# Decay steps pass one wait more in each mixing step, and half of the early head transfers are issued by GpSimd

## The chip, the cores and the metric

The kernel runs on one core of a Trainium2 chip. The metric is the device time of one execution in microseconds (us), and less is better. Three executions before the change took 908.11, 912.96 and 916.42 us; their median is 912.96 us.

## The reference

For 4 batches, 8 heads, 768 positions and a head size of 48, the reference runs a gated linear recurrence and then two token-and-channel mixers.

```python
mag = sqrt(a_re**2 + a_im**2)
scale = minimum(mag, 0.999) / (mag + 1e-6)            # a = a_re + i*a_im, times scale
for t in range(768):                                  # for each batch and head
    S_re, S_im = (Re(a_t * S) + outer(k_t, v_t), Im(a_t * S))
    y[t] = q_t @ S_re
x = y as [batch, 768, 384]
h = relu(x^T @ w_tok1) @ w_tok2;  u = x + h^T          # token mixing
u = u + relu(u @ w_ch1) @ w_ch2                        # channel mixing, first set
xn = (u - mean) / sqrt(var + 1e-6) * g
out = u + relu(xn @ w_ch1') @ w_ch2'                   # channel mixing, second set
```

## The kernel before

The recurrence is not run position by position. The running product of the decays is formed as a magnitude and an angle, and q and k are multiplied with it, so that each head becomes a few matmuls over chunks of 128 positions.

**Decay work** (`Piece`, driven by `gen_E`). The 384 rows (8 heads times 48) of a batch are three row tiles of 128 rows, and a piece is one row tile over one half of the positions. A piece goes through F (the magnitude; its first instruction is the Square of L228), G and H (running product, q and k scaled), T1 and T2 (running angle, sine and cosine) and T3. Nearly all of it is 384 columns wide: VectorE (DVE) through the recorder of L172, ScalarE (ACT) through `act` of L198, and three-element copies on GpSimd (POOL), L274 and L320 to L325. T3 ends with the transfers to the heads: rows of the piece are copied by DMA into the head tiles `stk`, one transfer from `R` (L338; named t, u or w in the trace) and one from `qkt` (L339; named qk or u). A row tile overlaps three or four heads, so a piece issues three or four pairs. All of them stand in the queue of SyncE (SP).

**Heads** (`gen_P`). A head comes in three parts: transposes of k (L507) and the first half of the scores (L520); the second half and the sums for the state (L547, scanned at L548); the output (L567 to L579). The results are split into two half-precision numbers (`xh`, `xl`, L475 and L476).

**Mixing** (`gen_M`). For each batch: `tok1` (with two `relu_split`, L670 on ACT and L672 on DVE), `tok2` (six chunks, each with an ACT and a DVE eviction, L721 and L722, and a Square, L725), then two rounds of `mlp(wm1)` and two of `mlp(wm2)`, 12 steps each. A step is 18 matmuls of 384 columns (`mm3`, L662 to L664) and one `relu_split`, so there are 198 of the L670 activations: 48 steps in each batch and two for each of three `tok1`.

**What sets the order.** The main loop takes one mixing step, then lets the decay work of the next batch run (`run_E`), and then up to two head parts (`run_P`). `run_E` has a budget, and it also stops at every "wait" that the decay generator yields; a piece yields seven of them. At the end of a batch all head parts of the next batch are forced out ahead of its `tok1`, with whatever decay work they need. The tile framework then arranges the emitted instructions on each engine by a timeline of its own, and each engine executes in that order. `tc.issue_after` adds an edge to that arrangement. The same framework gives DMAs their semaphores. `tokw` (L679) fetches the token weights of the next batch from POOL's queue as soon as the buffers are free.

Of the kernel before, what the change touches and what calls it, by code (L numbers as in the profile page):

```python
# [21 lines left out]
P = 128  # L22
# [16 lines left out]
def tile_kernel(ctx: ExitStack, tc: tile.TileContext, a_in, qk_in, v_in, aq2_in, v2_in, wt_in, wm1_in, wm2_in, w64_in, g_in, c_in, out):  # L39
# [150 lines left out]
    def act(**k):  # L190
        s = "trig" if k["func"] in (AF.Sin, AF.Arctan) else "logs"
        if tab["set"] != s:
            with ExitStack() as gates:
                for x in tab["ops"]:
                    gates.enter_context(tc.issue_after(x))
                tab.update(set=s, load=A.preload_act_table_set(sets[s]).ins, ops=[])
        with tc.issue_after(tab["load"]):
            tab["ops"].append(A.activation(**k).ins)  # L198

    class Piece:  # L200
# [21 lines left out]
        def F(self):  # L222
# [5 lines left out]
            A.activation(out=self.sq.rearrange("p (x s) -> p x s", x=2), in_=self.both, func=AF.Square)  # L228
# [84 lines left out]
        def T3(self, qkt):  # L313
# [12 lines left out]
            for k in range(self.n):  # L326
# [6 lines left out]
                while r < P:  # L333
# [5 lines left out]
                    nc.sync.dma_start(out=stk[b, h][D + d0:D + d0 + m, hf], in_=qkt[r:r + m, k])  # L339
# [5 lines left out]
    def gen_E():  # L345
        qks = [load_qk(0, j // 2, j % 2) for j in range(6)]
        load_w(1)
        ps = [[Piece(0, i, hf) for hf in range(2)] for i in range(3)]

# [98 lines left out]
    def gen_P(alt):  # L448
# [30 lines left out]
        for n, (b, h) in enumerate(heads):  # L479
# [20 lines left out]
            A.activation(out=dr.rearrange("p e (y c) -> p e y c", y=2), in_=kq[:, :, 2 * HB:].unsqueeze(1).to_broadcast([2 * D, D, 2, 3]), func=AF.Copy)  # L500
# [3 lines left out]
            for half in range(2):  # L504
                if half == 0:
                    for c in range(5):
                        T.transpose(tr[:, c * 96:(c + 1) * 96], qc(c, 1), eye[0:96, 0:96])  # L507
                    kTc = A.activation(out=kT, in_=tr[:, 0:480].rearrange("p (c d) -> p c d", c=5), func=AF.Copy, scale=(VS * SS if n in YS else 1.0) / (QS if n in QZ else 1.0))
# [16 lines left out]
                ev = V.tensor_tensor(out=sT[half], in0=sc[:, 0:3 * P].rearrange("p (c t) -> p c t", c=3), in1=pair(mask, 3), op=ALU.mult)  # L525
# [169 lines left out]
    def tok1_half(g, r1):  # L695
# [3 lines left out]
        for j in range(2):  # L699
# [4 lines left out]
            A.activation(out=r1[j][:, 0, cs], in_=p[:, j], func=AF.Relu, accum_out=hstat[:, n_h[0]:n_h[0] + 1])  # L704
# [320 lines left out]
    st = {"phase": "", "alt": True, "e": 0, "p": 0, "pp": 0, "w": 0, "need": 0, "c": 0, "mk": 0}  # L1025
# [24 lines left out]
    def run_E(budget, until=None):  # L1050

        if until is None and budget < 0:
            return
        while st["e"] < 3 * B and (until is None or st["e"] < until):
# [63 lines left out]
    for b in range(B):  # L1118
        k = 0
        while True:  # L1120
# [20 lines left out]
            run_E(EB if b else EB0 if k <= KE else EB1)  # L1141
# [38 lines left out]
PADB = 0  # L1180
PIPE = 0
# [38 lines left out]
EB = 2200  # L1220
# [5 lines left out]
NSTK = 5  # L1226
YS = [n for n in range(32) if n >= YH or n in YX]
# [51 lines left out]
```

## Time and profile before

| | |
|---|---|
| runs | 908.11, 912.96, 916.42 us |
| profiled execution | 912.68 us, its span 910.9 us |
| mean granted TensorE clock | 0.96 of full speed |
| PE busy | 816.8 us (90% of the span) |
| DVE busy | 631.2 us (69%) |
| ACT busy | 606.2 us (67%) |
| POOL busy | 97.8 us (11%) |

The profiled execution is one of its own, 0.28 us under the median of the runs. PE is TensorE's matmul side; its busy time counts a matmul as long at half clock as it lasts there, so that a busy PE at a granted clock of 0.50 does half of the work. The clock has two levels, 1.2 and 2.4 GHz, shown as 0.50 and 1.00 of full speed. ACT and DVE instructions overlap at their edges, so the distance between two starts on a full engine is a little under the duration of one.

### The profile page before, as it was taken

Reading aid. Unit: us, or ns where it says so; the run is one execution under the profiler, and the core shown is the slowest. Engines: PE = TensorE matmul, PEld = TensorE weight load, DVE = VectorE, ACT = ScalarE, POOL = GpSimd, SP = SyncE. Lnnn points to the kernel's source line nnn. Section 1 sums busy time; section 2 is a strip of 40 time slices with the busy share of each in tenths; the row PEclk is TensorE's granted clock in tenths of the full one; section 3 lists DMA queues with packets and bytes.
Section 4 is the critical chain, followed back from the end, with each engine's and each line's share of the span. In section 5 each row is a group of like instructions: output and inputs, shape, how many; then the busy total and the mean of one; then the engine's idle time right before and its main releaser. Section 6 shows DMA issues by size and latency. Waiting matters only on the chain.

```text
span 910.9 us, 15777 instructions
## 1 busy us (share of the span) xinstructions
PE 816.8 (90%) x5802; PEld 551.3 (61%) x5802; DVE 631.2 (69%) x1094; ACT 606.2 (67%) x1631; POOL 97.8 (11%) x171
## 2 busy tenths in 40 slices
PE   0079898999989999999999988999999999999996
PEld 0068775555757676666567755666567766655563
DVE  6786479998888988426789987336889642364533
ACT  8787147785578996627879996627779934464642
POOL 0421020311011001000020103000020000011110
PEclk9977799999999899999999986999999999999999
DMA  8634684155742642101524141100403011465662
GB/s 302 190 105 125 169 296 140 53 157 153 218 155 68 196 139 82 48 2 45 147 60 145 41 129 47 53 14 14 131 27 117 27 37 60 143 203 196 201 223 97
DMA packets 41606, 108.28 MB, mean 119 GB/s; under 512 B 5904, under 2 KB 23824, under 8 KB 41520
## 3 DMA queue, kind: packets, MB, share of 16 engines
q1 hardware_dynamic: 31936, 56.72, 20.9%
q0 software_dynamic: 9584, 50.47, 17.3%
q8 instruction: 47, 0.77, 0.4%
q14 instruction: 39, 0.32, 0.1%
HBM read 77.20 MB, written 11.01 MB: 97 GB/s over the span
## 4 chain that ended last, share of the span: by engine, by line
PE 34%; ACT 6%; DVE 6%; SPq 2%; issue 1%; DMA 1%; DVEq 0%; ACTq 0%
PE m L663 10%; PE m L664 10%; PE m L662 10%; ACT t L198 1%; PE sc L520 1%; DVE t L172 1%; DVE qk L172 1%; ACT hid L670 1%; SPq L338 1%; SPq L339 1%; PE tr L547 1%; DVE aj L172 1%; DVE xc L780 1%; DMA stk<-t 1%; PE m L719 0%
## 5 line engine op out<-in xcount | busy, mean ns | idle before, releaser
L672 DVE SCALAR_TENSOR_TENSOR hid<-m,hid 128x384 f16<-128x384 f32 x198 | 109.4, 554 | 149.2 <-ACT hid L670 148.6
L662 PE MATMUL m<-u,w 128*128 128x384 f16 x576 | 188.1, 327 | 1.4 <-DVE u L722 0.8
L663 PE MATMUL m<-u,w 128*128 128x384 f16 x576 | 188.0, 326 | 0.0
L664 PE MATMUL m<-u,w 128*128 128x384 f16 x576 | 188.0, 326 | 0.0
L670 ACT ACTIVATE hid<-m 128x384 f16<-128x384 f32 x198 | 95.5, 483 | 138.5 <-PE m L664 137.8
L663 PE MATMUL m<-hid,w 128*128 128x384 f16 x540 | 177.6, 329 | 3.0 <-DVE hid L672 2.7
L664 PE MATMUL m<-hid,w 128*128 128x384 f16 x540 | 177.6, 329 | 0.0
L662 PEld LDWEIGHTS <-w 128*128 128x128 f16 x1176 | 116.1, 99 | 84.6 <-issue 15.2
L664 PEld LDWEIGHTS <-w 128*128 128x128 f16 x1176 | 116.6, 99 | 80.2 <-issue 10.6
L663 PEld LDWEIGHTS <-w 128*128 128x128 f16 x1176 | 116.3, 99 | 76.3 <-issue 4.9
L662 PE MATMUL m<-hid,w 128*128 128x384 f16 x540 | 131.6, 328 | 9.1 <-ACT hid L670 8.3
L172 DVE SCALAR_TENSOR_TENSOR t<-t 128x384 f32<-128x384 f32 x80 | 44.1, 555 | 16.7 <-ACT t L228 12.0
L520 PE MATMUL sc<-stk 96*128 96x128 f32 x300 | 46.1, 288 | 1.6 <-DVE r L525 1.6
L595 POOL DMA_DIRECT2D raw<-in_wm x48 | 25.6, 534 | 174.9 <-DVE sq L640 83.2
L520 PEld LDWEIGHTS sc<-stk 96*128 96x128 f32 x300 | 41.5, 200 | 3.7 <-DVE r L525 1.8
L641 ACT ACTIVATE sq<-sq 128x768 f16<-128x768 uint8 x28 | 23.6, 843 | 28.4 <-DVE sq L640 28.4
L507 PE MATMUL m<-cst,stk 96*128 96x96 f32 x10 | 2.1, 348 | 45.0 <-DMA stk<-qk 45.0
L198 ACT ACTIVATE t<-t 128x384 f32<-128x384 f32 x80 | 40.6, 514 | 0.3
L615 ACT ACTIVATE w<-raw 128x768 f16<-128x768 f32 x28 | 25.3, 904 | 22.2 <-DVE raw L613 22.2
L670 ACT ACTIVATION_READ_ACCUMULATOR hid<-m 128x1 f32 x198 | 38.5, 195 | 0.0
L172 DVE TENSOR_TENSOR qk<-qk,t 128x768 f32<-128x768 f32 x40 | 38.1, 955 | 0.5
L612 DVE SCALAR_TENSOR_TENSOR pad<-raw 128x768 uint8<-128x768 uint8 x28 | 29.0, 1034 | 11.6 <-DMA raw<-in_wm 9.3
(281 smaller groups left out, 1713.7 us busy)
## 6 DMA issues: line engine op xcount, KB each, us to landing
raw<-in_wm POOLq DMA_DIRECT2D x48, 768.0 KB, 4.8
qk<-in_qk SPq DMA_DIRECT2D x23, 384.0 KB, 4.0
aj<-in_a SPq DMA_DIRECT2D x9, 768.0 KB, 5.0
stk<-t SPq DMA_DIRECT2D x40, 144.6 KB, 3.2
stk<-qk SPq DMA_DIRECT2D x40, 144.6 KB, 3.0
raw<-in_wt SPq DMA_DIRECT2D x6, 768.0 KB, 4.5
v<-in_v SPq DMA_DIRECT2D x32, 144.0 KB, 2.4
x_d<-xc SPq DMA_DIRECT2D x24, 192.0 KB, 3.5
```

Source lines behind the costliest of these rows:

```text
L172: r = getattr(nc.vector, n)(*a, **k)
L198: tab["ops"].append(A.activation(**k).ins)
L520: last = T.matmul(sc[:, (c % 3) * P:(c % 3 + 1) * P], qc(c, 1), qc(c, 0), start=True, stop=True)
L595: (nc.sync if n < NSY else nc.gpsimd).dma_start(out=raw.bitcast(U8), in_=w_src[n].bitcast(U8)[:, 3:3 + 8 * S])
L612: V.scalar_tensor_tensor(out=pad[0].bitcast(U8).rearrange("p (a b) -> p a b", b=4)[:, :, 3], in0=byte, scalar=3, in1=byte, op0=ALU.logical ...
L615: wact[n] = A.activation(out=dst[:, :, 0], in_=w, func=AF.Copy, scale=WS).ins
L641: A.activation(out=t[:, HB:2 * HB].bitcast(F16), in_=bad_, func=AF.Copy, accum_out=wstat[:, n:n + 1])
L662: T.matmul(out_, wh, xh_, start=first, stop=False)
L663: T.matmul(out_, wh, xl_, start=False, stop=False)
L664: T.matmul(out_, wl, xh_, start=False, stop=last)
L670: A.activation(out=hl[:, 0], in_=p, func=AF.Relu, accum_out=hstat[:, n_h[0]:n_h[0] + 1])
L672: last[:] = [V.scalar_tensor_tensor(out=hl[:, 1], in0=p, scalar=0.0, in1=hl[:, 0], op0=ALU.max, op1=ALU.subtract).ins]
```

## The change

Three settings differ; the other new names (`HOLD`, `AHOLD`, `FE`, `EBA`, `AHEAD`, `RW2`) have values under which the code does what it did.

- `EW = 2`: in the mixing of batches 1 and later, `run_E` stops at the second "wait" of a step, not at the first. The budget (2200) is as before. During the mixing of batch 0 it stops at the first.
- `DQ = ((0,0),(0,1))`: for row tiles 0 and 1 of batch 0 the transfers from `qkt` are issued by POOL. These are 6 and 8 transfers. Those from `R` stay on SP.
- `GSQ = 1`: in pieces of batches 1 to 3 the first Square of F is arranged behind the last activation that went through `act`.

```diff
@@ def F(self): @@
-            A.activation(out=self.sq.rearrange("p (x s) -> p x s", x=2), in_=self.both, func=AF.Square)
+            with tc.issue_after(tab["ops"][-1]) if b and GSQ else ExitStack():
+                A.activation(out=self.sq.rearrange("p (x s) -> p x s", x=2), in_=self.both, func=AF.Square)
@@ def T3(self, qkt): @@
-                    nc.sync.dma_start(out=stk[b, h][D + d0:D + d0 + m, hf], in_=qkt[r:r + m, k])
+                    (nc.gpsimd if (b, i) in DQ else nc.sync).dma_start(out=stk[b, h][D + d0:D + d0 + m, hf], in_=qkt[r:r + m, k])
@@ def run_E(budget, until=None): @@
+        waits = EW if st["bb"] else 1
...
             elif x == "wait":
-                if until is None:
+                waits -= 1
+                if until is None and waits <= 0:
                     return
@@ main loop @@
     for b in range(B):
         k = 0
+        st["bb"] = b
@@ settings @@
+GSQ = 1
...
+EW = 2
+DQ = ((0,0),(0,1))
```

The number of instructions of each kind on each engine is the same, 14 DMAs of SP being POOL's; what changes is their order. Three places show it. Lines of the changed kernel are some 3 to 15 higher than those of the kernel before (L670 is L685, L198 is L199, L339 is L342).

**ACT at the end of batch 1's mixing**, the rows up to the two `relu_split` of batch 2's `tok1` (`hid`). Before, its last twelve rows:

```order
L528 ACTIVATE hl<-r 128x384
L540 ACTIVATE junk,qstat<-qh 96x384
L528 ACTIVATE hl<-r 128x384
L475 ACTIVATE xh<-y 128x6x48
L540 ACTIVATE junk,qstat<-qh 96x384
L553 ACTIVATE junk,qstat<-vh 96x288
L515 ACTIVATE vh<-v 128x288
L551 ACTIVATE vh<-U 96x288
L477 ACTIVATE junk,ustat<-y 128x288
L537 ACTIVATE qh<-stk 96x768
L670 ACTIVATE hid,hstat<-m_6759 128x384
L670 ACTIVATE hid,hstat<-m_6760 128x384
```

and now, from the `relu_split` of the last mixing step on:

```order
L685 ACTIVATE hid,hstat<-m_6978 128x384
L522 ACTIVATE kT<-tr 128x480
L543 ACTIVATE hl<-r 128x384
L685 ACTIVATE hid,hstat<-m_7013 128x384
L685 ACTIVATE hid,hstat<-m_7014 128x384
```

Before, 43 activations (12 of decay, 31 of heads) stand between the last mixing step's `hid` and the first one of `tok1`; now two do.

**ACT and POOL at `tok2` of the next batch**, ACT from the second `hid` of batch 2's `tok1` on (`u` are the six evictions of `tok2`, `junk,ustat<-u` their Squares). Before:

```order
L670 ACTIVATE hid,hstat<-m_6760 128x384
L721 ACTIVATE u<-m_6819 128x384
L725 ACTIVATE junk,ustat<-u 128x384
L721 ACTIVATE u<-m_6837 128x384
L725 ACTIVATE junk,ustat<-u 128x384
L721 ACTIVATE u<-m_6855 128x384
```

and now:

```order
L736 ACTIVATE u<-m_7073 128x384
L740 ACTIVATE junk,ustat<-u 128x384
L231 ACTIVATE t<-aj 128x768
L199 ACTIVATE t<-aj 128x384 x2
L736 ACTIVATE u<-m_7091 128x384
L199 ACTIVATE t,rstat<-t 128x384
L199 ACTIVATE t<-t 128x384
L199 ACTIVATE t,rstat<-t 128x384
L740 ACTIVATE junk,ustat<-u 128x384
L736 ACTIVATE u<-m_7109 128x384
```

Up to the second mixing step's `hid`, 20 decay activations and three more of heads stand there beside the 18 of before. It is the same at `tok2` of batch 1: 19 decay activations, none before. On POOL the fetches of token weights stood next to each other; around batch 1's `tok2` there is now decay work between and behind them:

```order
L694 DMA tokw<-tokw_d 128x3072
L277 TENSOR_TENSOR pstat<-aj,t 128x3
L323 COPY t<-pstat 128x3
L323 COPY qk<-pstat 128x3
L277 TENSOR_TENSOR pstat<-aj,t 128x3
L327 COPY t<-pstat 128x2
L327 COPY qk<-pstat 128x2
L694 DMA tokw<-tokw_d 128x3072
L328 MEMSET t 128x1
L328 MEMSET qk 128x1
```

**SP and POOL at the start**, the transfers of row tile 0 (two halves) to heads 0 to 2 (`stk` twice, then `w`). SP before:

```order
L338 DMA stk<-t 48x771 x2
L338 DMA w_333<-t 32x771
L339 DMA stk<-qk 48x771 x2
L339 DMA w_333<-qk 32x771
L338 DMA stk<-t 48x771
L339 DMA stk<-qk 48x771
L338 DMA stk<-t 48x771
L339 DMA stk<-qk 48x771
L338 DMA w_333<-t 32x771
L339 DMA w_333<-qk 32x771
```

Now SP has the six of `t` alone, and POOL has, behind the three-element copies of that tile:

```order
L327 COPY qk<-pstat 128x2
L342 DMA stk<-qk 48x771 x2
L342 DMA w_333<-qk 32x771
L342 DMA stk<-qk 48x771 x2
L342 DMA w_333<-qk 32x771
```

## Rows read from the trace of the kernel before

**Rows 1.** The page, busy time by engine: us, share of the span, instructions

```profile
PE 816.8 (90%) x5802; PEld 551.3 (61%) x5802; DVE 631.2 (69%) x1094; ACT 606.2 (67%) x1631; POOL 97.8 (11%) x171
```

**Rows 2.** Stretches: length; PE, PEld, DVE, ACT, POOL busy; clock; DMA share; GB/s

```profile
45.00:156.10 111.10, 96.01 (x656) 80.74 (x657) 80.23 (x127) 63.47 (x154) 17.78 (x29) 0.83 0.56 172
239.50:348.70 109.20, 104.00 (x779) 76.60 (x779) 93.84 (x160) 91.05 (x242) 9.90 (x24) 0.95 0.49 143
357.70:373.60 15.90, 15.01 (x154) 11.08 (x153) 10.43 (x20) 11.69 (x36) 0.54 (x1) 1.00 0.38 117
373.60:478.30 104.70, 102.76 (x662) 62.97 (x661) 64.41 (x114) 63.46 (x180) 5.83 (x9) 1.00 0.20 60
478.30:539.50 61.20, 58.93 (x527) 42.45 (x525) 55.85 (x99) 60.96 (x174) 3.73 (x11) 1.00 0.38 108
539.50:565.50 26.00, 20.92 (x156) 14.91 (x156) 21.28 (x39) 20.64 (x65) 8.23 (x6) 0.61 0.11 35
565.50:577.80 12.30, 12.21 (x125) 8.32 (x121) 5.33 (x10) 9.47 (x31) 1.12 (x2) 1.00 0.35 112
577.80:740.60 162.80, 160.81 (x1236) 105.33 (x1234) 104.28 (x184) 113.41 (x336) 6.60 (x10) 1.00 0.17 49
740.60:749.40 8.80, 8.72 (x54) 5.04 (x52) 3.44 (x7) 1.03 (x4) 0.00 (x0) 1.00 0.15 58
```

**Rows 3.** Single stretches, columns as above

```profile
41.00:45.00 4.00, 0.02 (x1) 0.05 (x1) 0.51 (x1) 3.14 (x7) 0.00 (x0) 1.00 1.02 193
...
60.00:80.00 20.00, 19.15 (x101) 16.86 (x101) 14.84 (x24) 13.86 (x30) 3.81 (x8) 0.57 0.52 134
...
536.00:540.00 4.00, 2.19 (x15) 1.29 (x14) 2.79 (x6) 4.00 (x14) 0.00 (x0) 1.00 0.64 199
...
588.00:611.40 23.40, 23.40 (x146) 14.09 (x144) 4.49 (x9) 4.65 (x16) 0.00 (x0) 1.00 0.00 1
```

**Rows 4.** ACT in order of time, full: start, duration, line, operation

```profile
545.26 0.52 ACT L540 ACTIVATE junk<-qh 96x384 bf16<-96x384 f16 x1
...
545.78 0.51 ACT L528 ACTIVATE hl<-r 128x384 f16<-128x384 f32 x1
546.19 0.51 ACT L198 ACTIVATE t<-aj 128x384 f32<-128x384 f32 x1
```

**Rows 5.** Start of the program in order of time; brackets: idle before, releaser

```profile
40.56 0.96 DVE L172 TENSOR_TENSOR qk<-qk,t 128x768 f32<-128x768 f32 x1
...
41.54 0.53 SPq L338 DMA_DIRECT2D stk<-t  x1
...
42.98 0.50 SPq L339 DMA_DIRECT2D stk<-qk  x1
...
44.98 0.71 PE L507 MATMUL m<-cst,stk 96*128 96x96 f32 x3 [44.98 <-DMA stk<-qk]
```

**Rows 6.** Groups by line: busy, mean ns, idle before and releasers

```profile
L228 ACT ACTIVATE t<-aj 128x768 f32<-128x768 f32 x20 | 16.8, 840 | 11.7 <-DMA stk<-t 9.4 <-issue 1.0 <-DMA w<-t 0.9
```

**Rows 7.** SP in order of time, row tile 1's first and last of 16 transfers

```profile
65.66 1.78 SPq L338 DMA_DIRECT2D w<-u  x3
...
75.12 0.59 SPq L339 DMA_DIRECT2D w<-qk  x1
```

**Rows 8.** DMA issues: KB each, median us to landing

```profile
stk<-qk SPq DMA_DIRECT2D x40, 144.6 KB, 3.0
tokw_d<-w POOLq DMA_DIRECT2D x4, 384.0 KB, 2.7
```

**Rows 9.** Line 595: durations in ns, min/median/max, first and last start

```profile
L595 POOL DMA_DIRECT2D raw<-in_wm x48: 528/531/557, 26.5 to 889.7; - x48
```

**Rows 10.** POOL in order of time

```profile
56.70 2.95 POOL L320 COPY qk<-pstat 128x3 f32<-128x3 f32 x1
...
59.86 0.19 POOL L324 COPY w<-pstat 128x2 f32<-128x2 f32 x1
...
370.26 0.54 POOL L679 DMA_DIRECT2D tokw<-tokw_d  x1 [12.80 <-PE m L664]
```

More of the change, by code (lines that the diff above doesn't have):

```diff
@@ L359, in gen_E @@
             qk = qks[2 * i:2 * i + 2]
+            if i == 1 and FE & 1:
+                for x in each(p.F() for p in ps[2]):
+                    yield x
+            if i == 2 and FE & 2:
+                early.extend(Piece(1, 0, hf) for hf in range(2))
+                for x in each(p.F() for p in early):
+                    yield x
             for x in each(p.G() for p in ps[i]):
@@ L422, in gen_E @@
             for i in range(3):
-                ps = [Piece(b, i)] if WIDE else [Piece(b, i, hf) for hf in range(2)]
-                for x in run(p.F() for p in ps):
-                    yield x
+                ps = early if early and (b, i) == (1, 0) else [Piece(b, i)] if WIDE else [Piece(b, i, hf) for hf in range(2)]
+                if ps is not early:
+                    for x in run(p.F() for p in ps):
+                        yield x
                 qk = load_qk(b, i)
@@ L499, in gen_P @@
                 dr = ap.tile([2 * D, D, NCH], F32, tag="dr", name="dr", bufs=1)
-            A.activation(out=dr.rearrange("p e (y c) -> p e y c", y=2), in_=kq[:, :, 2 * HB:].unsqueeze(1).to_broadcast([2 * D, D, 2, 3]), func=AF.Copy)
+            with after(AHOLD.get(n)):
+                A.activation(out=dr.rearrange("p e (y c) -> p e y c", y=2), in_=kq[:, :, 2 * HB:].unsqueeze(1).to_broadcast([2 * D, D, 2, 3]), func=AF.Copy)
             tr = ps_(2)
@@ L507, in gen_P @@
                         T.transpose(tr[:, c * 96:(c + 1) * 96], qc(c, 1), eye[0:96, 0:96])
[L508 removed]
+                    with after(AHOLD.get(n)):
+                      kTc = A.activation(out=kT, in_=tr[:, 0:480].rearrange("p (c d) -> p c d", c=5), func=AF.Copy, scale=(VS * SS if n in YS else 1.0) / (QS if n in QZ else 1.0))
                     if n in YS:
@@ L524, in gen_P @@
                     sT.append(ap.tile([P, 3, P], F32, tag="sT", name="sT", bufs=NST))
-                ev = V.tensor_tensor(out=sT[half], in0=sc[:, 0:3 * P].rearrange("p (c t) -> p c t", c=3), in1=pair(mask, 3), op=ALU.mult)
+                with after(HOLD.get((n, half))):
+                  ev = V.tensor_tensor(out=sT[half], in0=sc[:, 0:3 * P].rearrange("p (c t) -> p c t", c=3), in1=pair(mask, 3), op=ALU.mult)
                 if n in YS:
@@ L1082, in run_P @@
             run_E(0, until=tiles_for(st["p"]))
+            for key in (HOLD.get((st["p"], 0)), HOLD.get((st["p"], 1)), AHOLD.get(st["p"])):
+                while key and key not in fin:
+                    x = nxt(E, "E")
+                    if isinstance(x, tuple) and x[0] == "done":
+                        st["e"] = x[1] * 3 + x[2] + 1
             st["pp"] += 1
@@ L1180 @@
 PADB = 0
+HOLD = {}
+AHOLD = {}
+RW2 = (2, 3) + tuple(range(8, 16))
+AHEAD = lambda n: min(15, n + 4) if 7 <= n < 12 else 3 if n < 2 else n + 1
+DQ = ()
+EW = 1
+EBA = 2200
+KA = 0
+FE = 0
+GSQ = 1
 PIPE = 0
```

15 lines of the change are left out of this document (9 added, 6 removed).

## The prediction

> **What bounds the kernel now.** The busy table on the page comes first [rows 1]: TensorE's matmul side (PE) is busy for 816.8 us of 910.9, the next engine, DVE, for 631.2. The change neither adds nor removes an instruction, so PE's work stays; only time in which PE is idle or at half clock can be won. The windows by stage show where that lies [rows 2]. Most of it is at the start (45 us without a matmul, then 15 us idle in 45 to 156), which decay work must feed, and in one place late: 539.5 to 565.5, the first `relu_split` pair of batch 2's token mixing (`tok1`). There PE is busy 20.92 of 26.0 us at a mean clock of 0.61, which is 20.92 x 0.61 = 12.8 us of full-speed work. The same step of batch 3 lasts 8.80 us with 8.72 busy. The mixing around it (577.8 to 740.6) loses 2 us in 163.
>
> Why there: from 478.3 to 539.5 ACT is busy 60.96 of 61.2 us [rows 2], and the ACT rows follow each other every 0.41 to 0.52 us, decay (L198) and heads (L528, L540) in turn [rows 4]. The decay of batch 2 is behind at the end of batch 1's mixing, and all of the rest, with the head parts that hang on it, is pressed ahead of `tok1`. From 536 to 540 PE is busy 2.19 of 4 us while ACT is busy 4.00 [rows 3], still at clock 1.00; a mean of 0.61 over the 26 us that follow means about 20 us at the lower level, 1.2 GHz. Earlier in a batch's mixing there is room: a stretch without head parts, 588 to 611.4, has ACT busy for 4.65 of 23.4 us [rows 3]. With a second wait in each step decay moves ahead into such steps.
>
> **The change part by part.** The sum goes against the profiled execution, 912.68 us, 0.28 below the median of the three runs.
>
> EW = 2, the pressed place. By the order, 43 ACT instructions stood between the last mixing step and `tok1` of batch 2; two do now. If the 26.0 us shrink to their full-speed work, the gain is 26.0 - 12.8 = 13.2. If only the idle 5.1 goes and the low clock stays, it is 5.1. The head matmuls that leave this place run elsewhere at full clock, so I don't take the 8.8 us of the twin as the goal. I take **-13** (bounds -13.2 and -5.1), since every stretch with PE at 98% or more in [rows 2] stands at clock 1.00. The stretch ahead, 478.3 to 539.5, has 2.3 us idle with ACT full; it has 34 decay and head activations fewer (decay 54 to 43, heads 57 to 34): **-1** (0 to -2.3). From 577.8 to 740.6 2.0 idle: **-1** (0 to -2).
>
> EW = 2 in batch 1's decay, 239.5 to 348.7. ACT is busy 91.05 and DVE 93.84 of 109.2; PE's 104.0 at clock 0.95 is 98.8 of work, 10.4 lost. By the order, 15 decay instructions of ACT and 10 of DVE fewer stand ahead of batch 1's `tok1`. At the spacing of 0.5 us of [rows 4] that is 7.5 us of ACT. **-4**, half, as neither engine is full (0 to -7.5).
>
> What receives the work. At `tok2` of batch 2 ACT has 41 instructions where it had 18. Its stretch, 565.5 to 577.8, has ACT at 9.47 of 12.3 us; 23 more at 0.46 are 10.6, so 20.1 of ACT beside PE's 12.21. If no matmul of heads moves in, that is 7.9 more; if enough do, nothing is lost. At `tok2` of batch 1 (357.7 to 373.6: ACT 11.69, PE 15.01) 19 decay activations come in, 8.7 at 0.46, so 20.4 against 15.9: 4.5. Bounds 0 and +12.4 for both. I take **+4**, nearer to none: the mixing of [rows 2] from 577.8 on carries ACT at 113.4 of 162.8 at a loss of 1%. The evictions L721 stand behind decay there, and PE waits for their PSUM buffers. On POOL the decay's `pstat` and its copies now stand behind the `tokw` fetches, of which one waited 12.80 us for PE [rows 10]; the decay instructions that need them are late by up to that, which costs only where heads wait. [...]
>
> The steps behind it, 373.6 to 478.3: ACT has 25 decay and 53 head instructions more, 78 x 0.51 = 39.8 on 63.46: 103.3 of 104.7. The head matmuls that come with them lengthen the stretch and shorten a later one. PE may wait at some steps: **+2** (0 to +5; the upper end is the idle time of PE, 5.2 of 109.2, where ACT and DVE are both loaded, 239.5 to 348.7).
>
> DQ, the start. Row tile 0's second half is ready when DVE's `qk` ends at 41.52; SP issues its first `qk` transfer at 42.98, behind others, and the first matmul starts on its landing, 44.98 [rows 5]. POOL's DMA instructions take 528 to 557 ns, 48 of them [rows 9], so POOL could issue it at 41.6, 1.4 us sooner. But from 41 to 45 the DMA engines are full, share 1.02 [rows 3]: there the queue that issues is not all of the limit. Landings from both queues are alike, 2.7 us for 384 KB from POOL and 3.0 for 144.6 KB from SP [rows 8]. Row tile 1's 16 transfers hold SP from 65.66 to 75.71 [rows 7]; with eight gone SP ends about 5 us sooner. In 60 to 80 PE is busy 19.15 of 20, at clock 0.57 [rows 3], so it waits for little. On the other side, POOL's transfers stand behind its own three-element copies, of which one took 2.95 us where others take 0.19 [rows 10]. Bounds -6.4 (1.4 + 5) and +6 (two such copies). **-2**.
>
> Added edge (GSQ). The 20 Squares of L228 waited 11.7 us in all, 9.4 of it for transfers (`stk<-t`) [rows 6], with ACT's queue held behind them. Behind the last activation they no longer go ahead of work that is ready; at most 9.4 comes free, and ACT is the limit only in the places counted above. A Square that is late delays its own piece; the next wait is then DVE's for it. **0**, its bounds within those of the terms above.
>
> Sum: -13 - 1 - 1 - 4 - 2 + 4 + 2 = **-15**, so 912.7 - 15 = **898 us**.
>
> **The rivals.**
>
> *The pressure only moves (no net change).* What is won at `tok1` of batch 2 is given back at `tok2` of both batches and in the steps behind: +12.4 and +5 in place of +4 and +2: 912.7 - 13 - 8 + 17.4 = **909**, up to 917 if the first term is only -5. For it: PE is at 98% in 373.6 to 478.3 and at 99% in 565.5 to 577.8, so decay put there has only little slack. Against it: PE has 13 us to recover at one place, and ACT room of 41 us in the stretch that receives most.
>
> [...]
>
> *GpSimd's issues are starved.* The copy of 2.95 us ran beside busy DVE. If each moved transfer took as long to issue, row tile 0's first head would start at 39.6 + 4 x 2.95 + 2 = 53.4 in place of 45, and row tile 1's last issue would end at 67.5 + 8 x 2.95 = 91 in place of 75.7. The first is lost whole, +8; of the second's +15 half, as PE has 19.15 of 20 us of work there: 898 + 2 + 15.5 = **916**. Against: none of the 48 POOL DMA instructions took over 557 ns [rows 9]. The Trainium skill, "SBUF — State Buffer", in its box on the "DVE blocks DMA" trap, states a rule against this edit: a DMA issued from GpSimd has its descriptors written by that engine's cores, and these are locked out while DVE runs an operation in a 2-port performance mode, which float32 tensor copies in SBUF trigger; the page advises the SP or ACT queue. By that rule the time would be near this rival's; the rows on POOL's own DMAs don't show it, though DVE is busy 69% of the span.
>
> *The change hardly does what it says.* EW counts waits, and the budget of 2200 may end a step first; the pressed place stays at 540. The order speaks against it (43 to 2). With the start's -2 alone, 911.
>
> **How the numbers follow.** Two runs of this kernel differ by up to 0.9%, so 1% (9.1 us, 903.8 to 922.1) is what can be told from no change. The forecast's case has 0.63. Its terms' distances to their ends, taken as independent, add (root of the sum of squares) to 7 us below 898 and 15 above; what lies beyond 908 is left to the rivals, so it is 891 to 908, 0.51 of it below 903.8 and 0.12 above. No net change 0.15; starved issues 0.05; `tok2` pressed once 0.05 and at both 0.10; no effect 0.02. Faster by over 1%: **0.51**. Within: 0.12 + 0.15 + 0.05 + 0.05 + 0.02 = **0.39**. Slower: **0.10**. Range **887 to 918**: the forecast's case with 4 us more at its low end, and all cases but the slower one, which leaves out that 0.10 and the edges.
>
> **What would show it.** Right: the clock stays at 1.00 from batch 1's last step through batch 2's `tok2`, and the `tok1` stretch lasts 9 to 15 us with no decay rows of ACT in it; both `tok2` stretches stay under 20 us; the first matmul starts at 43 to 46; POOL's DMA instructions on L342 last about 0.53 us. Wrong: a mean clock under 0.9 in either `tok2`; L736 waited for behind L199; POOL's DMA instructions at 2 us or more; a 26 us stretch with clock 0.6 elsewhere. Most of all, if head parts now run short of PE work earlier in batch 1 and the clock falls there, the 13 us are not won but moved.

## The result and the profile after

The changed kernel takes 898.12 us, the median of 20 runs (891.73 to 909.39); the kernel before takes 910.78 over 20 runs of its own (903.80 to 916.42). The ratio is 0.9861, with a 95% interval of 0.9841 to 0.9881. One of the changed kernel's runs, the 909.39, counts as slow and is left out of the ratio. The gain is 12.7 us, and the forecast of 898 us held.

The profiled execution of the changed kernel is its fastest, 891.73 us with a span of 889.9, while that of before is 1.9 us above its median. Of the 21 us between the two traces some 8 are therefore not the change's. A second trace of each kernel (e7 and e8 below: 899.02 and 913.35 us) shows in which stretches executions of one program differ.

The page of the changed kernel, busy time by engine, answers to [rows 1]:

```profile
PE 799.5 (90%) x5802; PEld 539.2 (61%) x5802; DVE 629.7 (71%) x1094; ACT 603.8 (68%) x1631; POOL 102.2 (11%) x185
```

PE's busy time is 17.3 us lower at the same number of matmuls: fewer of them ran at half clock.

The stages are cut below at the `relu_split` activations on ACT (`hid`), which are the same 198 in every kernel. They are numbered from 0: batch 0's mixing steps are 0 to 47, `tok1` of batch 1 is 48 and 49, batch 1's steps are 50 to 97, `tok1` of batch 2 is 98 and 99, batch 2's steps begin at 100. So the pressed place of the prediction ends at hid 98, and the two `tok2` lie between hids 48 and 50 and between 98 and 100. Windows of the changed kernel between hids 0, 16, 46, 48, 50, 70, 96, 98, 100 and 146, each with its length, busy time of PE, PEld, DVE, ACT and POOL (instructions), mean granted clock, DMA share and GB/s; the first row runs from 45 us to hid 0, and steps 0 to 16 are left out:

```profile
45.00:137.50 92.50, 81.73 (x611) 70.45 (x612) 71.50 (x112) 54.09 (x129) 17.20 (x36) 0.87 0.60 192
190.50:328.70 138.20, 133.73 (x959) 94.21 (x958) 121.08 (x202) 107.26 (x275) 18.61 (x34) 0.98 0.46 140
328.70:344.20 15.50, 13.97 (x108) 9.55 (x107) 13.55 (x26) 13.11 (x34) 0.38 (x3) 1.00 0.70 210
344.20:363.90 19.70, 15.00 (x157) 11.35 (x156) 19.40 (x35) 19.02 (x52) 6.02 (x8) 1.00 0.19 64
363.90:430.60 66.70, 65.61 (x446) 41.32 (x445) 47.68 (x84) 49.38 (x144) 2.94 (x8) 1.00 0.27 82
430.60:533.10 102.50, 98.63 (x825) 67.10 (x824) 88.64 (x157) 95.25 (x273) 12.56 (x18) 1.00 0.31 88
533.10:543.00 9.90, 9.90 (x64) 6.08 (x62) 4.93 (x10) 2.15 (x8) 0.00 (x0) 1.00 0.17 47
543.00:562.10 19.10, 16.51 (x163) 12.47 (x161) 14.36 (x29) 16.24 (x48) 1.31 (x4) 1.00 0.40 122
562.10:716.60 154.50, 154.42 (x1190) 100.71 (x1189) 91.23 (x161) 98.37 (x302) 4.27 (x8) 1.00 0.13 39
```

The same windows of the kernel before, cut at the same hids:

```profile
45.00:147.70 102.70, 88.56 (x611) 76.37 (x612) 71.83 (x115) 56.41 (x135) 17.25 (x28) 0.82 0.56 172
198.50:344.10 145.60, 138.25 (x979) 97.07 (x978) 128.67 (x213) 114.18 (x290) 15.67 (x36) 0.96 0.50 149
344.10:356.10 12.00, 11.47 (x86) 7.53 (x85) 11.04 (x20) 7.89 (x24) 3.12 (x6) 1.00 0.00 1
356.10:371.90 15.80, 14.91 (x156) 11.51 (x155) 11.47 (x23) 11.04 (x31) 1.12 (x2) 1.00 0.31 92
371.90:433.10 61.20, 61.20 (x404) 37.33 (x402) 26.82 (x47) 30.07 (x95) 0.00 (x0) 1.00 0.11 37
433.10:534.70 101.60, 98.70 (x775) 67.04 (x774) 90.62 (x160) 91.22 (x251) 9.36 (x18) 1.00 0.36 102
534.70:565.00 30.30, 23.90 (x170) 16.61 (x169) 24.66 (x45) 24.95 (x76) 8.43 (x8) 0.66 0.18 56
565.00:576.20 11.20, 11.11 (x120) 7.72 (x119) 4.77 (x9) 8.40 (x25) 1.12 (x2) 1.00 0.28 79
576.20:737.70 161.50, 159.51 (x1227) 104.56 (x1226) 104.28 (x184) 114.42 (x340) 6.60 (x10) 1.00 0.18 53
```

Lengths alone mislead, since head matmuls moved from one stretch to another. What can be compared is the time lost to PE: length less busy time times clock. It is an estimate, since the clock is the mean of the whole stretch, to two decimals. In the pressed place before (seventh row) it is 30.3 - 23.9 x 0.66 = 14.5 us; now 9.9 - 9.9 = 0. The place with a clock of 0.66 is gone, and from hid 46 to 146 no stretch is under 1.00.

Two windows of the changed kernel's second trace (e7), from 45 us to hid 0 and from hid 16 to 46:

```profile
45.00:142.60 97.60, 85.41 (x611) 72.74 (x612) 71.67 (x112) 54.41 (x129) 17.24 (x36) 0.84 0.58 183
195.80:335.50 139.70, 134.99 (x959) 95.27 (x958) 121.15 (x202) 107.18 (x275) 18.66 (x34) 0.96 0.45 139
```

and of the second trace of before (e8):

```profile
45.00:144.50 99.50, 85.20 (x611) 74.02 (x612) 71.49 (x114) 56.97 (x134) 17.28 (x28) 0.85 0.59 180
195.30:344.20 148.90, 140.25 (x981) 98.27 (x978) 128.89 (x213) 114.67 (x291) 15.70 (x36) 0.95 0.48 145
```

By the same working the first stretch loses 21.4 and 25.9 us in the two traces of the changed kernel and 30.1 and 27.1 in those of before: executions of one program differ there by 3 to 4.5 us. Between hids 16 and 46 they differ by 2.4 us (7.8 and 10.2) and 3.3 us (12.4 and 15.7). These four, and the column 16-46 further down, are sums over hids 16 to 32 and 32 to 46; the single rows above give 7.1, 10.1, 12.9 and 15.7, so up to 0.7 us of them is rounding. Behind hid 50 the two traces of each program agree in lost time to 0.2 us in every stretch. A difference of single traces counts as shown below only behind hid 46, or where it is well over 4 us.

At the start, the first matmul and the second half's transfers on POOL ahead of it (start, duration, engine, line; in brackets the idle time before and what ended it):

```profile
41.82 1.00 POOL L342 DMA_DIRECT2D stk<-qk  x2 [1.31 <-issue]
...
45.62 0.71 PE L520 MATMUL m<-cst,stk 96*128 96x96 f32 x3 [45.62 <-DMA stk<-qk]
```

The second half's transfer was issued 1.16 us sooner than in [rows 5], at 41.82, and the first matmul that waits for it came 0.64 us later, at 45.62: the earlier issue bought no earlier landing. The traces of the other runs agree. In the seven traces that have row tile 0's transfers on POOL the first matmul starts 2.9 to 3.9 us after that issue, at 45.5 to 46.4; in the seven that have them on SP 2.0 to 2.6 us after it, at 45.0 to 47.7. All 14 transfers of row tiles 0 and 1 on POOL, grouped by line (durations in ns, least, median, most):

```profile
L342 POOL DMA_DIRECT2D w<-qk x10: 488/504/524, 40.0 to 70.1; - x10
L342 POOL DMA_DIRECT2D stk<-qk x4: 502/513/550, 39.0 to 42.3; - x4
```

They take what [rows 9] gave, so none of the 14 issues was lengthened. The Trainium skill, "SBUF — State Buffer", in its box on the "DVE blocks DMA" trap, would have their descriptors held up while DVE runs in a 2-port mode, which a float32 copy in SBUF triggers. This trace hardly tests that rule: DVE ran beside 2.7 of the 7.2 us that the 14 issues took, and what it ran there were TENSOR_TENSOR instructions of two inputs, no copy. What did change is the time from issue to landing. Row tile 1's eight transfers from `qkt` have a median of 4.6 us here, and of 3.6 to 4.6 in all seven traces that have them on POOL; in the seven that have them on SP it is 2.6 to 2.7. SP's own eight beside them rise as well, from 2.7 in before to 3.4 here. Whether POOL's queue is slower or only more is under way at once stays open.

ACT at `tok2` of batch 2 in the changed kernel, in order of time, behind the first eviction (546.57) and its Square:

```profile
548.98 0.84 ACT L231 ACTIVATE t<-aj 128x768 f32<-128x768 f32 x1 [1.28 <-DMA stk<-t]
549.73 0.92 ACT L199 ACTIVATE t<-aj 128x384 f32<-128x384 f32 x2
550.56 0.47 ACT L736 ACTIVATE u<-m 128x384 f16<-128x384 f32 x1
```

The second eviction (L736) stands behind a Square that waits 1.28 us for a transfer, and behind the decay activations after it. PE's waits in this stretch and in that of batch 1 (344.2 to 363.9) by what ended them (us in all, times, longest) are

```profile
PE m L677 <- DVE u L737: 1.4, 2, 0.7
PE sc L534 <- DVE r L540: 1.2, 1, 1.2
```

and

```profile
PE m L677 <- DVE u L737: 3.6, 3, 1.7
PE m L677 <- DVE hid L687: 1.1, 1, 1.1
```

L737 is the DVE half of the same eviction, which follows ACT's. The two stretches lose 4.7 us at batch 1 and 2.6 at batch 2, and of that the evictions are 3.6 and 1.4. At batch 2 DVE's half waits for ACT's, 0.64 us at the second eviction. At batch 1 no such wait shows: the first three DVE halves start 0.7 to 1.9 us after ACT's half has ended, behind decay and head work on DVE itself. So there the evictions stand behind decay on both engines.

### The profile page after: what moved, and what is told of

It reads as the page before. It is cut to its first block, busy times and chain, and to the rows that moved or that the text cites. A ratio compares the mean times of both kernels' runs of the same rounds, so it can differ in the third digit from the quotient of the medians.

```text
span 889.9 us, 15744 instructions
## 1 busy us (share of the span) xinstructions
PE 799.5 (90%) x5802; PEld 539.2 (61%) x5802; DVE 629.7 (71%) x1094; ACT 603.8 (68%) x1631; POOL 102.2 (11%) x185
## 4 chain that ended last, share of the span: by engine, by line
PE 41%; ACT 10%; DVE 5%; DMA 2%; issue 1%; SPq 1%; DVEq 0%; ACTq 0%
PE m L678 12%; PE m L677 12%; PE m L679 12%; ACT t L199 2%; DMA stk<-t 1%; ACT hid L685 1%; PE sc L534 1%; PE tr L562 1%; DVE xc L795 1%; DMA v<-in_v 1%; DVE t L172 1%; DVE hid L687 1%; ACT junk L740 1%; DVE qk L172 1%; ACT t L300 0%
## 5 line engine op out<-in xcount | busy, mean ns | idle before, releaser
L685 ACT ACTIVATE hid<-m 128x384 f16<-128x384 f32 x198 | 95.5, 483 | 122.7 <-PE m L679 121.9
L534 PE MATMUL sc<-stk 96*128 96x128 f32 x300 | 44.3, 282 | 1.2 <-DVE r L540 1.2
L610 POOL DMA_DIRECT2D raw<-in_wm x48 | 25.6, 533 | 166.2 <-DVE sq L655 86.6
L520 PE MATMUL m<-cst,stk 96*128 96x96 f32 x10 | 2.1, 348 | 45.6 <-DMA stk<-qk 45.6
L199 ACT ACTIVATE t<-t 128x384 f32<-128x384 f32 x80 | 40.8, 515 | 1.2 <-DVE t L172 0.9
L277 POOL TENSOR_TENSOR pstat<-aj,t 128x3 f32<-128x3 f32 x20 | 27.2, 1358 | 118.2 <-DVE t L172 74.6
L685 ACT ACTIVATION_READ_ACCUMULATOR hid<-m 128x1 f32 x198 | 38.7, 195 | 0.0
```

The lines of the kernel that those rows point to most:

```text
L277: (nc.vector if ACP else G).tensor_tensor(out=pc, in0=n_end, in1=w_end, op=ALU.mult)
L534: last = T.matmul(sc[:, (c % 3) * P:(c % 3 + 1) * P], qc(c, 1), qc(c, 0), start=True, stop=True)
L610: (nc.sync if n < NSY else nc.gpsimd).dma_start(out=raw.bitcast(U8), in_=w_src[n].bitcast(U8)[:, 3:3 + 8 * S])
L685: A.activation(out=hl[:, 0], in_=p, func=AF.Relu, accum_out=hstat[:, n_h[0]:n_h[0] + 1])
```

## The experiments

All ratios are to the kernel before, run beside the kernel on the same chip. They are not the quotients of the two medians given with them, most of all in e4 (quotient 0.9960) and e6 (1.0103); the argument goes by the ratios and their intervals. Lost PE time is worked out as above from one trace each, between the hids in the column's head.

| kernel | EW | transfers on POOL | edge | ratio (95%) | 16-46 | 46-50 | 70-96 | 96-98 | 98-100 |
|---|---|---|---|---|---|---|---|---|---|
| before | 1 | none | no | 1 | 12.4 | 1.4 | 2.9 | 14.5 | 0.1 |
| changed | 2 | tiles 0, 1 | yes | 0.9861 (0.9841 to 0.9881) | 7.8 | 6.2 | 3.9 | 0 | 2.6 |
| e1 | 2 | none | no | 0.9922 (0.9896 to 0.9947) | 11.4 | 5.7 | 3.5 | 0 | 3.1 |
| e2 | 1 | tiles 0, 1 | no | 0.9992 (0.9968 to 1.0017) | 5.2 | 4.5 | 2.9 | 16.2 | 0.1 |
| e3 | 1 | none | yes | 1.0126 (1.0105 to 1.0147) | 10.4 | 4.1 | 6.0 | 12.5 | 5.2 |
| e4 | 2 | none | yes | 0.9937 (0.9914 to 0.9961) | 9.8 | 5.7 | 3.6 | 0 | 2.8 |
| e5 | 2 | tiles 0, 1 | no | 0.9874 (0.9823 to 0.9925) | 4.3 | 7.0 | 3.6 | 0 | 3.0 |
| e9 | 2 | tile 0 | no | 0.9873 (0.9841 to 0.9906) | 6.4 | 6.5 | 3.6 | 0 | 2.9 |
| e10 | 2 | tile 1 | no | 0.9875 (0.9833 to 0.9918) | 12.2 | 4.1 | 3.5 | 0 | 3.0 |

**e1, EW = 2 alone.**

```diff
-DQ = ((0,0),(0,1))
+DQ = ()
-GSQ = 1
+GSQ = 0
```

> EW = 2 alone; the transfers and the edge of the first Square are as before. Theory A (EW carries the gain: the pressed place before tok1 of batch 2 goes, -14.5 us in the two traces, and 6 us come back at the two tok2): about 901 to 904 us where before has 911, a ratio of 0.989 to 0.993; in the profile the stretch from the last mixing step's hid to the first hid of batch 2's tok1 lasts 9 to 12 us (before 30.4, changed kernel 9.9), and each tok2 stretch (second hid of tok1 to the next hid) 17 to 20 us (before 15.8 and 11.2, changed kernel 19.6 and 19.1); the first mixing hid stays near 147. Theory B (the start carries more than I forecast: the first mixing hid comes 10.2 us sooner in the changed kernel's trace, by the transfers on GpSimd's queue): EW alone gives 906 to 908.

Measured: 902.65 us against 909.0, 0.9922. Windows between hids 16 and 46, at `tok2` of batch 1, in the pressed place and at `tok2` of batch 2:

```profile
194.20:338.60 144.40, 136.50 (x980) 96.78 (x978) 128.25 (x213) 114.09 (x291) 15.64 (x36) 0.98 0.50 150
...
352.20:371.50 19.30, 14.16 (x146) 10.57 (x146) 18.40 (x33) 16.60 (x43) 2.31 (x5) 1.00 0.68 181
...
539.50:549.60 10.10, 10.10 (x65) 6.19 (x64) 4.86 (x10) 2.09 (x7) 0.00 (x0) 1.00 0.16 44
549.60:568.90 19.30, 16.16 (x163) 12.37 (x162) 14.52 (x30) 16.41 (x49) 1.31 (x4) 1.00 0.43 139
```

Theory A holds: the pressed place is gone at full clock, both `tok2` pay, and the balance is 7.1 us (0.78% of 909.0; the interval is 4.8 to 9.5 us, and the medians differ by 6.4). That is about half of the gain or somewhat more, and not all of it: the intervals of e1 and of the changed kernel don't overlap. The first row says something more: between hids 16 and 46 DVE and ACT are busy as before, 128.25 and 114.09 us against 128.67 and 114.18. EW = 2 does nothing there.

**e2, the transfers alone.** EW = 1 and GSQ = 0, DQ as changed.

> Half of the transfers of row tiles 0 and 1 on GpSimd's queue, alone. Theory A: within 3 us of before (a ratio of 0.997 to 1.003). Theory B: 904 to 907, a ratio near 0.994, and the first mixing hid at 138 to 142. Theory C (the 10 us at the start are the clock's lot in single executions, not a gain of either edit): no change in the time, and the first mixing hid anywhere from 137 to 149, in before's own repeated profile too. On starved issues: the 14 DMA instructions of GpSimd take 0.50 to 0.56 us each by A, B and C, 2 us or more by the rival.

Measured: 908.43 against 909.0, no change. Windows between hids 0, 16, 46 and 50, and in the pressed place:

```profile
145.50:200.00 54.50, 47.68 (x274) 27.14 (x273) 52.91 (x79) 40.90 (x96) 10.23 (x12) 0.97 0.41 119
200.00:338.40 138.40, 133.19 (x967) 93.68 (x964) 116.88 (x195) 103.83 (x267) 16.34 (x33) 1.00 0.43 130
338.40:370.50 32.10, 27.62 (x256) 20.06 (x256) 30.27 (x55) 28.37 (x79) 5.83 (x10) 1.00 0.48 147
533.30:565.70 32.40, 23.78 (x169) 15.84 (x168) 24.78 (x45) 25.10 (x76) 7.95 (x8) 0.68 0.16 52
```

Theory B falls; A and C both fit, with the first mixing hid at 145.5. But the transfers do change something far from where they stand: between hids 16 and 46 DVE has 116.88 us of work where before had 128.67, and 5.2 us are lost in place of 12.4. By the order 15 decay instructions of ACT have left that stretch and 16 more stand at `tok1` and `tok2` of batch 1. As I read it, the framework's timeline has other queues to reckon with and arranges decay later. In this trace 7.2 us are won there, and 3.5 are given back between hids 0 and 16, 3.1 between 46 and 50 and 1.7 in the pressed place.

**e3, the edge alone.** EW = 1, DQ = (), GSQ = 1.

> The edge that puts the first Square of F behind the last activation, alone. Theory A: no change, 0.997 to 1.003, the pressed place of 26 to 31 us before tok1 of batch 2 still there. Rival: the 3.7 us less of loss ahead of batch 1's tok1 come from it, and the time falls by 3 to 4 us, a ratio near 0.996.

Measured: 921.55 against 909.0, **slower by 1.26%**; both theories fall. Windows from hid 84 to the pressed place, in it, at `tok2` of batch 2, and ahead of batch 3's `tok1` (hids 132 to 148):

```profile
476.80:534.20 57.40, 53.00 (x461) 36.77 (x461) 47.50 (x87) 53.84 (x152) 6.26 (x12) 0.97 0.30 87
534.20:560.60 26.40, 17.07 (x145) 10.61 (x143) 21.04 (x37) 22.95 (x63) 6.16 (x7) 0.81 0.35 98
560.60:580.40 19.80, 17.66 (x153) 13.36 (x154) 17.27 (x33) 16.27 (x48) 4.30 (x7) 0.83 0.20 72
681.20:755.00 73.80, 69.34 (x641) 49.19 (x640) 54.00 (x97) 60.10 (x178) 3.07 (x7) 1.00 0.20 53
```

The pressed place has spread: the clock is low at `tok2` of batch 2 too, 0.83 where before had 1.00, and in the last stretch 73.8 - 69.34 = 4.5 us are lost ahead of batch 3, where before lost none. From hid 46 to 146 this trace loses 11.4 us more than that of before: less in the pressed place itself, and 5.0 more between hids 84 and 96, 5.1 at `tok2` of batch 2 and 4.5 ahead of batch 3. As I read it, a Square that may not go ahead of ready work starts its piece later, and with one wait in each step nothing makes up for it.

**e4, the change without the transfers.** EW = 2, GSQ = 1, DQ = ().

> The change without the transfers on GpSimd's queue (EW = 2 and the edge). Theory A: as the changed kernel within 3 us, a ratio of 0.985 to 0.990 to before. Theory B: 4 to 6 us above the changed kernel, a ratio of 0.991 to 0.994.

Measured: 905.37 against 909.0, 0.9937. Theory B is nearer. The intervals of e4 and of the changed kernel don't overlap, so with EW = 2 and the edge the transfers are worth about 0.76%, 7 us, and alone nothing. Where those 7 us lie, e4's window between hids 16 and 46 helps to say:

```profile
204.90:345.90 141.00, 133.14 (x959) 93.54 (x957) 121.08 (x202) 107.23 (x275) 18.64 (x34) 0.99 0.46 137
```

DVE, ACT and POOL have as many instructions there as in the changed kernel, 202, 275 and 34, and as much work, though no transfer of e4 is on POOL. So the edge alone arranges this stretch as the changed kernel has it (e3, with DVE at 120.1 us, has it too), and e4 loses 9.8 us there, between the 7.8 and 10.2 of the changed kernel's two traces. From hid 46 to 146 e4 and the changed kernel both lose 13.9 us. What the transfers win beside the edge must then lie ahead of hid 16, by these traces: to hid 0 e4 loses 34.3 us, the changed kernel 21.4 and 25.9. That is not a measure of the 7 us, since e4's trace is of its slowest run, 4.4 us over its median.

**e5, the change without the edge.** EW = 2, DQ as changed, GSQ = 0.

> The changed kernel without the edge on the first Square (EW = 2 and the transfers on GpSimd's queue). Theory A (the edge only delays decay: alone it cost 12 us; with EW = 2 there is slack and it costs little): 893 to 898 us, 0 to 4 us under the changed kernel, a ratio to before of 0.982 to 0.987. Rival (edge and transfers each only pay together with the other: EW alone 0.992, EW and edge 0.994, all three 0.986): 901 to 904, a ratio of 0.991 to 0.994.

Measured: 896.62 against 909.86, 0.9874. Against the changed kernel that can't be told apart, so the edge, which costs 1.26% alone, costs nothing that shows with EW = 2. That is theory A's reading; the rival's 0.991 is still inside the interval.

**e6, decay held out of `tok2`.** It takes away the forecast's +4, by two edits together: the first Squares are arranged behind `tok2`, and in a mixing step decay doesn't run past the next batch.

```diff
+            held = fin.get(("t2", b - 1)) if self.i < HT else None
-            with tc.issue_after(tab["ops"][-1]) if b and GSQ else ExitStack():
+            with tc.issue_after(held) if held is not None else tc.issue_after(tab["ops"][-1]) if b and GSQ else ExitStack():
...
-                A.activation(out=junk, in_=uh[:, c, ts], func=AF.Square, ...)
+                fin["t2", b] = A.activation(out=junk, in_=uh[:, c, ts], func=AF.Square, ...).ins
...
-        while st["e"] < 3 * B and (until is None or st["e"] < until):
+        while st["e"] < (3 * B if until is not None else min(3 * B, 3 * st["bb"] + 6)) and (until is None or st["e"] < until):
...
+HT = 1
```

> The changed kernel with the decay of batches 2 and 3 held out of tok2: in a mixing step the decay doesn't run past the next batch, and the first Squares of batch b's row tile 0 are arranged behind the last Square of batch b-1's tok2. By the order 3 decay instructions of ACT stand in each tok2, where the changed kernel has 19 and 17. Theory A (decay on ACT at tok2 costs 4.7 and 2.6 us of PE time there, and nothing later): each tok2 stretch loses under 1 us, and the time falls 5 to 8 us under the changed kernel, a ratio to before of 0.977 to 0.981. Rival (decay that starts later is late later, as with the edge alone): a pressed place with a clock under 0.9 ahead of tok1 of batch 2 or 3, and 900 to 910 us.

Measured: 919.23 against 909.86, 1.0151 (1.0096 to 1.0206). Windows at `tok2` of batches 1 and 2, and of the steps behind each (hids 70 to 84, 100 to 132, and in the last row 50 to 70):

```profile
345.00:357.70 12.70, 11.51 (x94) 7.52 (x92) 5.88 (x12) 9.96 (x27) 1.23 (x3) 1.00 0.34 116
...
430.90:495.90 65.00, 57.83 (x461) 38.93 (x459) 52.43 (x94) 59.77 (x170) 4.84 (x10) 0.97 0.35 102
550.40:563.00 12.60, 11.41 (x93) 7.45 (x92) 5.80 (x12) 9.84 (x27) 1.21 (x3) 1.00 0.40 136
563.00:690.10 127.10, 115.81 (x875) 75.29 (x875) 111.73 (x196) 117.58 (x317) 16.06 (x23) 0.99 0.24 66
357.70:430.90 73.20, 68.12 (x470) 41.94 (x470) 63.01 (x109) 65.72 (x174) 11.77 (x14) 0.98 0.27 76
```

Each `tok2` now loses 1.2 us, a little over theory A's 1. The time is beyond what either said, 919 where the rival had 900 to 910, and the rival's pressed place ahead of `tok1` isn't there. Its cause is: the work comes back in the steps behind, where ACT is busy for 90% to 93% of the time and DVE for 81% to 88%. PE is busy 57.83 of 65.00 us between hids 70 and 84, 115.81 of 127.10 between 100 and 132 and 68.12 of 73.20 between 50 and 70, each at a clock a little under 1.00; the changed kernel lost 2.0, 0.1 and 1.1 us there. The 6 us at the two `tok2` are what early decay costs, and cheaper than late decay as these two edits make it; which of the two does the harm isn't separated.

**e7 and e8, the same two programs once more.** No edit.

> The changed kernel once more, for a second trace of the same program. Theory A (where the three edits don't reach, single executions differ): from 45 us to the first mixing hid it loses 21 to 32 us of PE time, not the 21.4 of the first trace again, while from batch 1's step 2 on it is as the first trace within 1 us. Theory B (the start's gain belongs to the change): 20 to 23 us.

> The kernel before once more, for a second trace. Theory A: from 45 us to the first mixing hid it loses 21 to 34 us where the first trace lost 30.1, and the pressed place before tok1 of batch 2 loses 12 to 16 us again. Theory B: 29 to 31 us at the start.

Measured: 25.9 us lost to hid 0 in e7 (21.4 in the first trace), 27.1 in e8 (30.1). Theory A holds and theory B falls for both. In e8 the pressed place loses 14.6 us, as before's 14.5.

**e9 and e10, row tile 0's or row tile 1's transfers.** EW = 2, GSQ = 0, DQ = ((0,0),) and DQ = ((0,1),).

> EW = 2, no edge, and only row tile 0's six transfers from qkt on GpSimd's queue. By the order this alone gives the arrangement that both tiles give: 19 and 72 decay instructions of ACT in steps 16 to 32 and 32 to 46 of batch 0's mixing, against 26 and 80 without any transfer on GpSimd. Theory A (the transfers pay because the arrangement of batch 0's mixing is another, not because a queue is relieved): as with both tiles, 895 to 899 us, a ratio of 0.984 to 0.989, and 4 to 6 us of PE time lost between hids 16 and 46. Theory B (SP's relief pays, most of it in row tile 1, whose 16 issues held SP for 10 us): 900 to 904, a ratio near 0.991.

> EW = 2, no edge, and only row tile 1's eight transfers from qkt on GpSimd's queue. By the order the arrangement of batch 0's mixing is as without (26 and 80). Theory A: as EW = 2 alone, 901 to 904 us, a ratio of 0.990 to 0.994, and 10 to 13 us lost between hids 16 and 46. Theory B: 895 to 899.

Windows between hids 16 and 46, of e9

```profile
198.50:337.20 138.70, 133.77 (x958) 93.73 (x956) 118.09 (x197) 103.97 (x268) 16.78 (x33) 0.99 0.43 132
```

and of e10

```profile
192.10:337.10 145.00, 136.33 (x970) 96.36 (x969) 128.16 (x212) 113.83 (x289) 15.00 (x36) 0.98 0.51 150
```

The stretch does what theory A said: e9 has the new arrangement (DVE 118.09, 6.4 us lost), e10 the old one (128.16, 12.2). The times don't follow: 0.9873 and 0.9875. Neither theory is shown. In e10's trace 24.6 us are lost before hid 0 (e1: 26.7) and 4.1 between 46 and 50 (e1: 5.7), but the first is within what two executions differ by. Why row tile 1's transfers alone seem to pay stays open; the intervals of e1 and e10 overlap, so it may be nothing.

**e11, EW = 2 in batch 0's mixing too.** DQ as changed, GSQ = 0.

```diff
-        waits = EW if st["bb"] else 1
+        waits = EW
```

> EW = 2 in the mixing of batch 0 too, with both tiles' transfers on GpSimd's queue and without the edge. By the order steps 16 to 32 have 66 decay instructions of ACT (19 before), 32 to 46 have 59 (72), and 4 (16) stand at tok1 of batch 1. Theory A (the same relief as in batch 1's mixing): 4 to 7 us lost between hids 16 and 50 where the kernel without it lost 11.4, so 890 to 894 us, a ratio of 0.978 to 0.983. Rival (the first steps of batch 0's mixing are already loaded by the weights' work, DVE at 57 of 65 us, and 47 decay instructions more make a pressed place there): 900 to 908.

Measured: 918.39 against 910.21, 1.0091 (1.0056 to 1.0126). The window between hids 16 and 32:

```profile
190.90:301.80 110.90, 98.85 (x598) 71.64 (x597) 92.28 (x147) 74.54 (x179) 13.84 (x27) 0.85 0.49 148
```

The rival's pressed place is there, and it costs more than the rival's 900 to 908. DVE has 92.28 us of work in it, 110.90 - 98.85 x 0.85 = 26.9 us are lost, where e5 lost 2.3, and 2.1 us between hids 46 and 50, where e5 lost 7.0, are no match.

**e12, idle matmuls in before's pressed place.** The kernel before, with

```diff
+                if b == 1 and k >= WK:
+                    warm(WN, psum("y", 1))
...
+WN, WK = 8, 42
```

behind each head part of the steps.

> The kernel before with 40 idle matmuls of 384 columns added, whose result nothing reads: 32 of them stand in PE's order among the head matmuls ahead of batch 2's tok1, 8 within it; ACT, DVE and all else are ordered as before. They are 6.5 us of work at full clock. Theory A (of the 14.5 us lost there about 8 are the half clock, which follows the dry stretch at 536 to 540): the mean clock between hids 96 and 98 is 0.85 or more where before had 0.66, and the time falls 3 to 7 us, a ratio of 0.992 to 0.997. Rival 1 (the clock falls all the same, from PE's pauses between heads): no gain, or up to 6 us slower. Rival 2 (the fill delays the heads that ACT waits for): the stretch gets longer at full clock, 0 to 4 us slower.

Measured: 916.74 against 910.21, 1.0069 (1.0047 to 1.0092). The pressed place, hids 96 to 98:

```profile
534.70:571.50 36.80, 27.80 (x209) 17.17 (x208) 25.21 (x45) 25.89 (x77) 3.57 (x8) 0.86 0.14 46
```

The mean clock is 0.86, as theory A said, and the stretch is 6.5 us longer. The fill ran from 544.6 on, behind the dry stretch. One idle matmul lasts 0.326 us, but the next starts 0.162 us after it, as the first three show:

```profile
544.64 0.65 PE L458 MATMUL y<-cst,eye_h 128*128 128x384 f16 x3 [0.44 <-ACT junk L489]
```

So the 40 are the 6.5 us of work at full clock that the expectation had, and 9.7 us as they ran, 16 of them at half clock: the clock fell again, from 553.8 to 560.7, as rival 1 had it. The fill stands in PE's queue among the heads, and the stretch grew by about the fill's own work. Theory A's gain is not there, but with the fill in the way of the heads e12 doesn't show what a better clock alone would be worth. ACT and DVE have about as much work as before, 25.89 and 25.21 us, and are no longer full with it over 36.80 us. What speaks for ACT and DVE as the limit are rows of before in the middle of its stretch:

```profile
546.00:550.00 4.00, 3.24 (x19) 2.84 (x16) 4.00 (x9) 4.00 (x14) 0.00 (x0) 0.50 0.21 79
554.00:558.00 4.00, 2.34 (x36) 1.70 (x36) 4.00 (x9) 3.97 (x15) 3.94 (x3) 0.50 0.02 4
```

DVE and ACT are full there and PE at half clock still pauses. How much of the 14.5 us the clock alone is worth stays open.

## Why the prediction was right

The time, 898, and the direction were right, and the largest term was right in place, size and cause. Of the smaller ones one had the wrong cause, and others the wrong size. That 898 came out to the microsecond is luck: the gain forecast was 15 us and the measured one is 12.7, and the sum started from 912.7, where the kernel before has a median of 910.8 over 20 runs.

- **The pressed place, -13.** Measured -14.5, in both traces of the changed kernel and in each kernel with EW = 2, and in none with EW = 1. The cause I gave, decay and heads pressed ahead of `tok1`, holds, since EW = 2 alone (e1) takes them out and the loss with them; in the middle of the place DVE is as full as ACT. How much of the loss is the half clock, of which I made much, e12 doesn't settle.
- **`tok2`, +4.** Measured +6.3 in the first traces (+3.8 and +2.5). The term was too small by 2.3. The mechanism was in the main as written: evictions behind decay are 5.0 us of PE's waits in the two stretches. DVE, which I left out, is as full as ACT at batch 1: 19.40 and 19.02 of 19.70 us. With 1.0 at `tok1` of batch 1 the term is 7.3.
- **Batch 1's decay, -4.** Measured -4.6 (12.4 to 7.8; in the second traces -5.5, 15.7 to 10.2), little more than two executions differ by, but the cause was wrong. I put it down to EW = 2, which doesn't apply in batch 0's mixing, where this stretch lies: e1 has the old arrangement and 11.4 us lost. Either of the other two edits makes the move, the transfers (e2) or the edge (e3, e4). The order had shown it, and I gave it to the wrong one of three edits, because I looked at the order of the whole change alone.
- **The start, -2.** Not settled, and perhaps too small. Of its two parts the 1.4 us did not come: the earlier issue won no earlier landing. The other did as an issue time: SP is through with row tile 1 at 69.9 us in place of 75.7. Whether PE gains by it single traces can't say, as two executions of one program differ there by 3 to 4.5 us. All 14 traces together point to a gain: from 45 us to hid 0 the eight with any transfers on POOL lose 21.4 to 27.7 us, 25.1 in the mean, the six without 25.6 to 34.3, 29.0 in the mean. The ranges overlap and the programs differ otherwise, so this is a hint. The rearrangement between hids 16 and 46 doesn't explain what the transfers are worth: e4 has it without them at 0.9937, and e10 has them without it at 0.9875, though e10's interval overlaps that of e1.
- **The edge, 0.** Right within the change (e5 against it), for a reason I didn't give: alone it costs 11.5 us by the ratio, 12.5 by the medians, and EW = 2 hides that. The sentence that a late Square only delays its own piece was wrong; the delay ran through to batch 3.
- **The other steps.** Hids 50 to 84 (373.6 to 478.3 before): +2 forecast, +1.1 measured. Hids 84 to 96: -1 forecast, +0.9 measured, though ACT is no longer full there. Hids 100 to 146: -1 forecast, -1.9 measured.

From hid 46 on, the first traces differ in lost time by +4.8 (hids 46 to 50), +1.1, +0.9, -14.5, +2.5 (`tok2` of batch 2) and -1.9, in sum -7.1 us, which is what e1's ratio gave for EW = 2. What is left of the 12.7 us, 5.6, must come from ahead of hid 46; that it needs the transfers is what e4 shows, and by what way is open. The rival in which the pressure only moves was true in part: of the 14.5 us, 9.3 came back between hids 46 and 100, more than the forecast's 6 and less than that rival's 17.4. No issue of GpSimd was lengthened.

The signs named for a right forecast all came: the clock at 1.00 through batch 2's `tok2`, 9.9 us with no decay on ACT at `tok1`, 19.7 and 19.1 us at the two `tok2`, the first matmul at 45.6, and POOL's issues at 0.49 to 0.55 us. One sign named for a wrong one came too: L736 stands behind L199 at both `tok2`. That is what the +4 had allowed for, and it cost more. A clock under 0.9 in a `tok2` came only in e3, which has EW = 1.

None of the experiments beats the changed kernel beyond its interval. e5, without the edge, ties with it.

## What to carry to other kernels

When one engine is the bound, look for the stretch where it is idle or slow while others are full, and cost the change in time lost to the bound engine, since lengths of stretches move with the work in them. Where a scheduler arranges the instructions, a change of three settings is three changes: compare the order for each of them alone before giving a term to one. Side work that starts early may cost a little where it lands and still be cheaper than the same work late, as holding it back (e6) showed. It has to land where there is room: put into steps that were already loaded (e11) it cost more than it saved.

## What was not expected of the hardware

Idle matmuls that raised TensorE's mean clock from 0.66 to 0.86 in a stretch (e12) did not shorten it; it grew by 6.5 us, about their own work. Executions of one program differ by 3 to 4.5 us in the stretch from 45 us to hid 0 and agree to 0.2 us behind hid 50. A transfer issued 1.16 us sooner on another queue, where [rows 3] had the DMA engines full, landed no sooner: over 14 traces the first matmul came 2.9 to 3.9 us after an issue on POOL and 2.0 to 2.6 us after one on SP. Row tile 1's eight transfers from `qkt` took 3.6 to 4.6 us to land (medians) when POOL issued them, and 2.6 to 2.7 when SP did.
